# Projection of q and k in two passes of 1024 tokens, the first by seven products of halves

## The chip, the cores and the metric

The kernel runs on one core of a Trainium2 chip. The metric is the device time of one execution in microseconds; the time of a kernel is the median of its runs. TensorE (PE) multiplies matrices, VectorE (DVE), ScalarE (ACT) and GpSimd (POOL) work on elements, and SyncE (SP), ScalarE and GpSimd issue DMAs, each in the order of the program.

## The reference

Two blocks read the same x (2048 tokens of 1024) and are mixed by a gate. Block A is attention with 32 heads of 32; block B chooses one of 64 experts for each of 32 heads by a product of keys.

```
qkv = x @ wqkv                                   # 1024 -> 3 x 1024: q, k, v of 32 heads
p   = softmax(q k^T * 32**-0.5);  a = (p v) @ wo
s1, s2 = (x w_q) split in halves, times k1, k2   # 8 scores each, the largest of each chosen
b   = sum over heads of gelu(x . u[e]) v[e]      # e: the chosen expert of the head
g   = sigmoid(sum(x * gate_w));   out = g * a + (1 - g) * b
```

This text is about q and k alone: x (2048 x 1024) times the first 2048 columns of `wqkv`.

## The kernel before

One program, one core. All products that need more accuracy than a rounded operand gives are made of two parts: `split(hi, lo, src)` (L92 to L94) copies a tile into a rounded type on ScalarE (L93: the high part) and subtracts it from the source on VectorE (L94: the low part). A product is then three matmuls: high by high, high by low, low by high. A matmul takes a 128x128 block of weights and 512 tokens.

The stages follow one another on TensorE: projection of q and k, router (`router_mm`, L394), v (`values`, L636), v again as seven products of halves for most tokens (`Halves.product`, L617), attention (scores L969, exponentials L979, p v L990), and the output projection.

Projection. x comes transposed, in eight block rows of 128 by 2048, and stays in SBUF as `xh` and `xl` (four tiles of 512 tokens each). The weights of q and k are 16 chunks of 128 columns: chunk c of q, then chunk c of k. The first two chunks run row by row while x arrives: for each block row `kc`, 24 matmuls into eight banks (L213). Their weights come on ScalarE's queue in four pieces (block rows 0, 1, 2 to 3, 4 to 7). The order on ScalarE and VectorE is that of the program: for `kc` 1, `split_x(1)` and then the third piece of the weights; for `kc` 2, `split_x(2)` and then the fourth piece; so both stand ahead of the next row of x.

The other 14 chunks run one after another: a chunk has four blocks of 512 tokens, each of 24 matmuls into one bank (L329). After a block, `evac` splits the bank into parts (L93, L94), takes the maximum of the high part (L141) and puts off the two stores to DRAM to the next eviction. Between the blocks stand other pieces of work, in a table by block number: `fold` (L274) folds the router's weights with its keys on TensorE, `gate` (L313) adds x times the gate's weights on VectorE, and near the end the router's folded weights are loaded and split. Eight banks of PSUM (`bk0` to `bk7`) are handed out in turn by `bank()`.

The loop over chunks before (L322 to L334; `whl` holds a chunk's two parts, `load_w` and `split_w` fetch and split the next):

```
for k, (w, c) in enumerate(chunks):
    hi, lo = whl.pop((w, c))
    for n in range(NQ):
        ps = bank()
        for kc in range(KC):
            for a, b, first, last in ((hi, xh, kc == 0, False), (hi, xl, False, False),
                                      (lo, xh, False, kc == KC - 1)):
                nc.tensor.matmul(ps, a[:, kc, :], b[n][:, kc, :], start=first, stop=last)
        if n == 0 and 0 < k < len(chunks) - 1:
            split_w(*chunks[k + 1])
        ...
        evac(w, c, n, ps, pair(ev, "", 1))
```

On GpSimd stand only the router's products (L408, L421, L434) and DMAs, the folds' stores among them.

`Halves` (before, after the router) makes a product of a 2x2 arrangement of halves by seven products in place of eight: A are the stationary blocks, B the moving ones.

```
FACTORS = dict(P1=("A11", "B11"), P2=("A12", "B21"), P3=("S4", "B22"), P4=("A22", "T4"),
               P5=("S1", "T1"), P6=("S2", "T2"), P7=("S3", "T3"))
S1 = A21 + A22, S2 = S1 - A11, S3 = A11 - A21, S4 = A12 - S2
T1 = B12 - B11, T3 = B22 - B12, T2 = B22 - T1, T4 = B21 - T2     # each overwrites one of its inputs
C11 = P1 + P2; u2 = P1 + P6; u3 = u2 + P7; u2 += P5; C22 = u3 + P5; C12 = u2 + P3; C21 = u3 + P4
```

Each product is 12 matmuls (four block rows, three parts) into one bank. S and T are sums of raw halves and are split into parts after that.

Of the kernel before, what the change touches and what calls it, by code (L numbers as in the profile page):

```python
# [16 lines left out]
S = 2048  # L17
# [14 lines left out]
def gated_mha_peer_kernel(ctx, tc, xT, wqkv, wv, wo, wq, k12, ug, v, out):  # L32
# [62 lines left out]


    xp = Pool("xp")

    xh, xl = ([xp.tile([128, KC, 512], F32R, name=f"x{part}{n}") for n in range(NQ)] for part in "hl")
    ps1 = Pool("ps1", space=PSUM)  # L100
    bank_no = [0]

    def bank():
        i = bank_no[0] % 8
        bank_no[0] += 1
        return ps1.tile([128, 512], F32, name=f"bk{i}")

    amax = const.tile([128, 2, KC], F32, name="amax")
    wp = Pool("wp", bufs=2)
    ev = Pool("ev", bufs=3)  # L110
    xr = Pool("xr", bufs=4)

    wraw, whl = {}, {}

    def load_w(which, c):
        t = wp.tile([128, KC, 128], F32, name="wraw", bufs=1)
        dma(t, wqkv[which * 8 + c].rearrange("p (k m) -> p k m", k=KC))
        wraw[which, c] = t

    def split_w(which, c):  # L120
        t = wraw.pop((which, c))
        hi = wp.tile([128, KC, 128], F32R, name="whi")
        lo = wp.tile([128, KC, 128], F32R, name="wlo")
        split(hi, lo, t)
        whl[which, c] = hi, lo
# [9 lines left out]
    def evac(which, c, n, ps, parts):  # L135

        m = parts[0].shape[1] // 512
        hi, lo = (t[:, n % m * 512:(n % m + 1) * 512] for t in parts)
        split(hi, lo, ps)
        mx = ev.tile([128, 1], F32, name="m", bufs=8)  # L140
        nc.vector.tensor_reduce(mx, hi.bitcast(F32), axis=AX.X, op=OP.max, apply_absolute_value=True)  # L141
        am = amax[:, which, c:c + 1]
        if n == 0:
            nc.vector.tensor_copy(am, mx)
        else:
            nc.vector.tensor_max(am, am, mx)
        store_parts()
        if n % m == m - 1:
            for dst, t in zip(QKD[which], parts):
                stores.append((dst[128 * c:128 * c + 128, (n + 1 - m) * 512:(n + 1) * 512], t))  # L150

    def pair(pool, name, m):
        return [pool.tile([128, m * 512], F32R, name=part + name) for part in ("hi", "lo")]
# [13 lines left out]
    x_t = {}  # L167

    def load_x(kc, pieces=1):
        t = xr.tile([128, S], F32, name="xraw")  # L170
        n = S // pieces
        for i in range(pieces):
            dma(t[:, i * n:(i + 1) * n], xT[kc * 128:(kc + 1) * 128, i * n:(i + 1) * n])
        x_t[kc] = t

    def split_x(kc):
        for n in range(NQ):
            split(xh[n][:, kc, :], xl[n][:, kc, :], x_t[kc][:, n * 512:(n + 1) * 512])

    w0 = []  # L180
    for w in range(2):
        w0.append([xr.tile([128, KC, 128], F32, name="w0raw", bufs=2),
                   wp.tile([128, KC, 128], F32R, name="whi"), wp.tile([128, KC, 128], F32R, name="wlo")])

    def load_w0(k0, k1):
        for w in range(2):
            dma(w0[w][0][:, k0:k1, :],
                wqkv[w * 8, :, k0 * 128:k1 * 128].rearrange("p (k m) -> p k m", m=128), nc.scalar)

    def split_w0(k0, k1):  # L190
        for raw, hi, lo in w0:
            split(hi[:, k0:k1, :], lo[:, k0:k1, :], raw[:, k0:k1, :])

    load_w0(0, 1)
    load_x(0, 4)
    load_w0(1, 2)
    load_x(1, 2)
    split_w0(0, 1)
    split_x(0)
    load_w0(2, 4)  # L200
    load_x(2, 2)
    load_w0(4, KC)
    load_x(3, 2)
    split_w0(1, 2)
    b0 = {(w, n): bank() for w in range(2) for n in range(NQ)}


    for i in range(9):
        nc.tensor.matmul(b0[1, NQ - 1][:, :128], ident, ident, start=True, stop=True)

    def mm0(w, n, kc, i):
        a, b = ((1, xh), (1, xl), (2, xh))[i]
        nc.tensor.matmul(b0[w, n], w0[w][a][:, kc, :], b[n][:, kc, :],  # L213
                         start=(kc == 0 and i == 0), stop=(kc == KC - 1 and i == 2))

    for kc in range(KC):
        if kc:
            split_x(kc)
        if kc in (1, 2):
            split_w0(2 * kc, 2 * kc + 2 if kc == 1 else KC)  # L220
        if kc + 4 < KC:
            load_x(kc + 4)
        if kc == KC - 5:
            load_w(0, 1)
        if kc == KC - 1:
            split_w(0, 1)
            load_w(1, 1)

            xr.close()
            ev0 = Pool("ev0")  # L230
        order = [(n, i) for i in range(3) for n in range(NQ)]
        if kc in (0, KC - 1):
            order = [(n, i) for n in range(NQ) for i in range(3)]
        for w in range(2):
            for n, i in order:
                mm0(w, n, kc, i)
            if kc == KC - 1:
                parts = pair(ev0, str(w), NQ)
                for n in range(NQ):
                    evac(w, 0, n, b0[w, n], parts)  # L240

    split_w(1, 1)
    load_w(0, 2)
    ev0.close()
    wqp = Pool("wqp", bufs=4)


# [315 lines left out]

    class Halves:

# [856 lines left out]
```

## Time and profile before

| | us |
|---|---|
| median of 3 runs | 1852.09 (1851.99 to 1853.69) |
| the profiled execution | 1852.0 |
| its span, first to last instruction | 1850.2 |
| first matmul of L213 | 6.67 |
| first matmul of L329 | 51.94 |
| first matmul of L394 (router) | 391.02 |

In the rows, a line number is one of the kernel before. A row of the timeline has the start and the length in us, the engine, line, operation, tile written and read, and behind it in brackets how long the engine sat idle before it and what ended that. A row of groups has the count, busy time, mean length in ns and idle time before. A row of stretches has the bounds, the length, and the busy time and count of TensorE, its weight loads, VectorE, ScalarE and GpSimd, then TensorE's granted clock, the DMA share and GB/s. Matmuls overlap, so the length of one is not its cost.

### The profile page before, as it was taken

How to read it: one execution, taken by the hardware profiler on the slowest of the kernel's cores; microseconds unless marked ns; L12 is line 12 of the kernel's file. 1: busy time of each engine (PE TensorE's matmuls, PEld its weight loads, DVE VectorE, ACT ScalarE, POOL GpSimd, SP SyncE). 2: the span in 40 equal slices, each digit the busy share in tenths (PEclk: the TensorE clock that was granted, in tenths of full speed). 3: DMA queues.
4: the chain of work that ended last, by engine and by line, in shares of the span. 5: the costliest groups of instructions: out<-in, count | busy, mean ns of one | idle time of the engine just before them, and what ended most of it. 6: DMA issues, size and time to landing. Idle time of an engine off the chain costs nothing.

```text
span 1850.2 us, 26111 instructions
## 1 busy us (share of the span) xinstructions
PE 1842.3 (100%) x10127; PEld 1128.0 (61%) x10127; DVE 1365.0 (74%) x1219; ACT 1197.8 (65%) x1491; POOL 172.3 (9%) x218
## 2 busy tenths in 40 slices
PE   9999999999999999999999999999999999999999
PEld 7877777887888744444444444444444444447887
DVE  4522224978887788888888888888888888895684
ACT  4211111201233399999999999999999999993221
POOL 0000000026401100000000000000000000001000
PEclk9999999999999999999999999999999999999999
DMA  5777784423237787767777777877777777866961
GB/s 216 283 255 252 273 291 135 133 69 104 80 119 249 253 184 160 174 157 173 164 174 176 167 183 159 191 162 182 174 165 173 162 179 164 181 146 192 279 185 63
DMA packets 122150, 332.10 MB, mean 179 GB/s; under 512 B 15924, under 2 KB 56260, under 8 KB 97768
## 3 DMA queue, kind: packets, MB, share of 16 engines
q1 hardware_dynamic: 85112, 180.72, 32.0%
q0 software_dynamic: 17904, 112.99, 28.3%
q10 hardware_dynamic: 19008, 36.71, 6.3%
q8 instruction: 80, 1.31, 0.3%
q14 instruction: 46, 0.38, 0.1%
HBM read 158.65 MB, written 72.10 MB: 125 GB/s over the span
## 4 chain that ended last, share of the span: by engine, by line
PE 94%; DMA 4%; SPq 1%; ACT 1%; issue 0%; DVE 0%; ACTq 0%; DVEq 0%
PE ring L969 27%; PE o L990 25%; PE bk L329 17%; PE bk L617 6%; PE pa L617 5%; PE bk L394 5%; PE bk L636 2%; PE bk L213 2%; DMA accd<-P 2%; PE bk L274 2%; PE ring L1003 1%; DMA wo_raw<-t1l 1%; SPq L75 1%; DMA out<-rb 1%; PE pa L1181 1%; DMA at<-atd 0%
## 5 line engine op out<-in xcount | busy, mean ns | idle before, releaser
L979 ACT ACTIVATE P<-ring 128x512 f32<-128x512 f32 (+2 forms) x1030 | 912.5, 985 | 15.1 <-DMA accd<-P 2.3
L1019 DVE TENSOR_TENSOR acc<-acc,P 128x2048 f32<-128x2048 f32 x319 | 731.0, 2292 | 74.2 <-ACT P L979 48.6
L990 PE MATMUL o<-P,V 128*32 128x512 f32 x3840 | 464.8, 599 | 0.0
L969 PE MATMUL ring<-Q,K 98*128 98x512 f32 x1024 | 272.3, 407 | 0.2
L969 PE MATMUL ring<-z,z 98*128 98x512 f32 x1020 | 271.3, 407 | 0.3 <-ACT P L979 0.2
L969 PEld LDWEIGHTS ring<-Q,K 98*128 98x128 f32 x1024 | 181.9, 188 | 144.7 <-ACT P L979 73.8
L969 PEld LDWEIGHTS ring<-z,z 98*128 98x128 f32 x1020 | 181.2, 188 | 143.8 <-ACT P L979 71.6
L990 PEld LDWEIGHTS o<-P,V 128*32 128x32 f32 x3840 | 98.8, 109 | 223.1 <-issue 214.4
L93 ACT ACTIVATE hi<-bk 128x512 fp32r<-128x512 f32 x64 | 37.6, 598 | 243.1 <-PE bk L329 231.8
L94 DVE TENSOR_TENSOR lo<-bk,hi 128x512 fp32r<-128x512 f32 x64 | 44.1, 690 | 182.7 <-ACT hi L93 178.1
L329 PE MATMUL bk<-xh,whi 128*128 128x512 f32 x448 | 176.2, 393 | 0.1
L329 PE MATMUL bk<-xh,wlo 128*128 128x512 f32 x448 | 174.4, 389 | 0.0
L329 PE MATMUL bk<-xl,whi 128*128 128x512 f32 x448 | 174.4, 389 | 0.0
L1012 POOL DMA_DIRECT2D accd<-P x95 | 81.5, 858 | 930.6 <-ACT P L979 400.9
L1017 DVE TENSOR_TENSOR acc<-P,P 128x2048 f32<-128x2048 f32 x32 | 73.4, 2292 | 74.1 <-ACT P L979 74.1
L329 PEld LDWEIGHTS bk<-xh,whi 128*128 128x128 f32 x448 | 84.1, 188 | 24.2 <-issue 6.7
L329 PEld LDWEIGHTS bk<-xh,wlo 128*128 128x128 f32 x448 | 84.1, 188 | 17.7
L329 PEld LDWEIGHTS bk<-xl,whi 128*128 128x128 f32 x448 | 84.2, 188 | 17.0
L1022 DVE TENSOR_TENSOR acc<-acc,accd 128x2048 f32<-128x2048 f32 x32 | 73.1, 2284 | 0.0
L979 ACT ACTIVATE accd<-ring 128x1024 f32<-128x1024 f32 (+2 forms) x64 | 62.3, 1034 | 1.7 <-PE ring L969 1.6
L617 PE MATMUL pa<-woh,acc 128*128 128x512 f32 x192 | 62.6, 390 | 0.3 <-DVE acc L94 0.3
L398 ACT ACTIVATE xu<-bk 128x64 f32<-128x64 f32 x16 | 3.6, 224 | 76.5 <-PE bk L394 71.6
(247 smaller groups left out, 1864.7 us busy)
## 6 DMA issues: line engine op xcount, KB each, us to landing
accd<-P POOLq DMA_DIRECT2D x95, 1024.0 KB, 7.4
wqt<-in_wq SPq DMA_DIRECT2D x32, 1024.0 KB
z<-kdh SPq DMA_DIRECT2D x32, 256.0 KB
z<-qdh SPq DMA_DIRECT2D x32, 256.0 KB
V<-vd SPq DMA_DIRECT2D x32, 256.0 KB
K<-kdh SPq DMA_DIRECT2D x32, 256.0 KB
Q<-qdh SPq DMA_DIRECT2D x32, 256.0 KB
od<-osb SPq DMA_DIRECT2D x32, 256.0 KB
```

The lines of the kernel that those rows point to most:

```text
L93: nc.scalar.activation(hi, src, AF.Copy)
L94: (on or nc.vector).tensor_tensor(out=lo, in0=src, in1=hi.bitcast(F32), op=OP.subtract)
L329: nc.tensor.matmul(ps, a[:, kc, :], b[n][:, kc, :], start=first, stop=last)
L394: nc.tensor.matmul(ps, a[t // 4][:, kc, tok], b, start=first, stop=last)
L617: nc.tensor.matmul(ps, self.a[a][i][:, k, :], self.b[b][j][k], start=(not first and k == 0 and i == j == 0), stop=(k == HC - 1 and i == 1))
L969: on_ring(nc.tensor.matmul(ring[:, i, :], K[:98, kt * 128:(kt + 1) * 128], Q[:98, qc * 512:(qc + 1) * 512], start=True, stop=True), i)
L979: on_ring(nc.scalar.activation(P[h, kt][:, q0 * 512:(q0 + m) * 512].rearrange("p (a m) -> p a m", a=m), ring[:, i:i + m, :], AF.Exp, scale ...
L990: nc.tensor.matmul(O[h][32 * qc:32 * qc + 32, :], Vt[g][:, kt, 32 * j:32 * j + 32], p[:, qc * 512:(qc + 1) * 512], start=(kt == 0), stop=( ...
L1012: nc.gpsimd.dma_start(ACCD[h], P[h, kt], accum_op=OP.add)
L1017: nc.vector.tensor_add(ACC[h], P[h, 0], P[h, kt])
L1019: nc.vector.tensor_add(ACC[h], ACC[h], P[h, kt])
L1022: nc.vector.tensor_add(ACC[h], ACC[h], ACCD[h])
```

## The change

The first pass covers tokens 1024 to 2047. Chunk 0 of q and k runs as before, row by row, for these tokens (four banks, 12 matmuls per block row). Then come seven units: unit c makes chunk c of q and of k together by the seven products of `Halves`. A11 and A12 are the two halves (512 of the 1024 input features each) of q's chunk, A21 and A22 those of k's; B11 and B12 are tokens 1024 to 1535 and 1536 to 2047 of the first 512 features, B21 and B22 of the others. The sums S run on GpSimd in every unit, 512 wide. T1, T2 and T4 run on GpSimd once, 2048 wide, T3 on VectorE. While a unit runs, the operands of the next are split, each when the product that last used its place is issued.

The second pass covers tokens 0 to 1023 for all 16 chunks in blocks of 24 matmuls as before; x of these tokens is loaded during units 6 and 7, the weights are loaded and split again, and x of the first pass is loaded and split again, since its raw blocks were overwritten by the T. The gate's terms, its sums on TensorE (before: in the router stage) and most folds move into the second pass, 12 folds into units 2 to 5. `evac` writes each block's maximum to a place of its own, and one reduction at the end replaces the running maximum.

The core of the diff (`Halves` itself moves up; its `sums` takes an engine and the places to write to):

```diff
+    def evac_hi(which, c, n, src):
+        hi, lo = (ev.tile([128, 512], F32R, name=part) for part in ("hi", "lo"))
+        nc.scalar.activation(hi, src, AF.Copy)
+        late.append((which, c, n, src, hi, lo))
+
+    def evac_lo():
+        which, c, n, src, hi, lo = late.pop(0)
+        nc.vector.tensor_tensor(out=lo, in0=src, in1=hi.bitcast(F32), op=OP.subtract)
+        nc.vector.tensor_reduce(amax4[:, which, c, n:n + 1], hi.bitcast(F32), axis=AX.X, op=OP.max,
+                                apply_absolute_value=True)
+        store_parts()
...
+    load_x(raws[0], 0, 0, T0, 2)
+    load_w0(1, 2)
+    load_x(raws[0], 0, 1, T0, 2)
+    split_w0(0, 1)
+    split_x(0)
+    load_w0(2, 4)
+    load_x(raws[0], 0, 2, T0)
+    load_w0(4, KC)
+    load_x(raws[0], 0, 3, T0)
+    split_w0(1, 2)
+    for k in range(HC):
+        load_x(raws[1], 1, k, T0)
+    w1 = [load_w(w, 1) for w in range(2)]
...
+    for kc in range(KC):
+        if kc:
+            split_x(kc)
+        if kc == 1:
+            split_w0(2, 4)
+        if kc == 2:
+            split_w0(4, KC)
+        if kc == 4:
+            t1 = x_sum("T1", nc.gpsimd)
+        order = [(n, i) for i in range(3) for n in (2, 3)]
+        if kc in (0, KC - 1):
+            order = [(n, i) for n in (2, 3) for i in range(3)]
+        for w in range(2):
+            for n, i in order:
+                mm0(w, n, kc, i)
...
+    set_rows(1)
+    t3 = x_sum("T3", nc.vector)
+    for name in ("S3", "S1"):
+        hq.sums(name, nc.gpsimd)
+    for name in ("A11", "A12"):
+        hq.parts(name)
+    for name in ("S2", "S4"):
+        hq.sums(name, nc.gpsimd)
+    t2, t4 = (x_sum(name, nc.gpsimd) for name in ("T2", "T4"))
+    x_parts("T3", t_tile("xh0"), t3)
+    hq.parts("S4")
+    x_parts("T1", t_tile("xl0"), t1)
+    hq.parts("S3")
...
+    evac_first(2)
+    hq.parts("S1")
+    x_parts("T2", t_tile("xh1"), t2)
+    hq.parts("S2")
+    evac_first(2)
+    x_parts("T4", t_tile("xh3"), t4)
+    hq.parts("A22")
+
+    def qk_unit(c, order, nxt, hooks):
+        p, done = {}, set()
+        k0 = 3 if c == 1 else 0
+        for k, name in enumerate(order):
+            if nxt and k == k0:
+                set_rows(nxt)
+                for s in ("S3", "S1"):
+                    hq.sums(s, nc.gpsimd)
+            p[name] = hq.product(name)
+            if name == "P1":
+                c1 = cp.tile([128, 512], F32, name="c1")
+                nc.scalar.activation(c1, p[name], AF.Copy)
+                if late:
+                    evac_lo()
+            if nxt and k == k0:
+                hq.parts("A11")
+                hq.sums("S2", nc.gpsimd)
...
+            if name == "P6":
+                u2, u3, u5 = (cp.tile([128, 512], F32, name=name) for name in ("u2", "u3", "u5"))
+                tt(u2, c1, p["P6"])
+                tt(u3, u2, p["P7"])
+                tt(u2, u2, p["P5"])
+                tt(u5, u3, p["P5"])
+                evac_hi(1, c, 3, u5)
+            if "P6" in p:
+                for q, (o, w, n) in (("P2", (c1, 0, 2)), ("P3", (u2, 0, 3)), ("P4", (u3, 1, 2))):
+                    if q in p and (w, n) not in done:
+                        done.add((w, n))
+                        tt(o, o, p[q])
+                        evac_hi(w, c, n, o)
+                        evac_lo()
+            if nxt and k >= k0:
+                for q in ("P7", "P5", "P6", "P2", "P3", "P4"):
+                    if q in p and q not in done:
+                        done.add(q)
+                        hq.parts(hq.FACTORS[q][0])
+                        if q == "P2":
+                            hq.sums("S4", nc.gpsimd)
...
+            store_parts()
+            for f, *args in hooks.get(name, ()):
+                f(*args)
...
+    hooks[7] = {"P1": [(load_raws, 1, "xh2")], "P7": [(w_chunk, 0, 0, 0), (again, 0, 0, "xh0")],
+                "P5": [(again, 0, 1, "xl0")], "P6": [(w_chunk, 1, 0, 1)],
+                "P2": [(again, 1, 0, "xh1")], "P3": [(again, 1, 1, "xl1")]}
+    for c in range(1, KC):
+        qk_unit(c, ("P1", "P2", "P3", "P7", "P5", "P6", "P4") if c == 1 else
+                ("P1", "P7", "P5", "P6", "P2", "P3", "P4"), c + 1 if c < KC - 1 else None, hooks[c])
...
+    between[1] = [(again2, 3, 1, "xl3", 1)]
+    between[2] = [(gate_raw, 3, 1, 1), (load_again, 2, 1, 1)]
...
+    order = [(0, 0), (1, 0), (0, 1), (1, 1)] + [(k, n) for k in range(2, len(chunks)) for n in range(2)]
+    for blk, (k, n) in enumerate(order):
+        w, c = chunks[k]
+        t = pairs[k % 2]
+        ps = bank()
+        for kc in range(KC):
+            for a, b, first, last in ((0, 0, kc == 0, False), (0, 1, False, False),
+                                      (1, 0, False, kc == KC - 1)):
+                nc.tensor.matmul(ps, t[:, kc // HC, a, kc % HC], x_at(b, n, kc), start=first, stop=last)
+        if blk == 2 or (blk > 3 and n == 0 and k < len(chunks) - 1):
+            nxt = 2 if blk == 2 else k + 1
+            w_chunk(*chunks[nxt], nxt % 2)
...
+        evac(w, c, n, ps)
```

`x_sum` makes one T in place over one of its inputs, `x_parts` splits it (2048 wide), `again` and `again2` split a reloaded block of x (2048 wide), `gate_raw` and `gate_part` add its gate terms (four operations of 512), `w_chunk` splits a reloaded chunk of weights (1024 wide).

507 lines of the change are left out of this document (285 added, 222 removed).

## The prediction

> **What bounds the kernel now.** I read the page first (busy shares, slices, the chain that ended last), then TensorE's waits and the timeline of the projection, then VectorE's, ScalarE's and GpSimd's rows, and last the loads of the start.
>
> ```profile
> span 1850.2 us, 26111 instructions
> PE 1842.3 (100%) x10127; PEld 1128.0 (61%) x10127; DVE 1365.0 (74%) x1219; ACT 1197.8 (65%) x1491; POOL 172.3 (9%) x218
> PE ring L969 27%; PE o L990 25%; PE bk L329 17%; PE bk L617 6%; PE pa L617 5%; PE bk L394 5%; PE bk L636 2%; PE bk L213 2%; DMA accd<-P 2%; PE bk L274 2%; PE ring L1003 1%; DMA wo_raw<-t1l 1%; SPq L75 1%; DMA out<-rb 1%; PE pa L1181 1%; DMA at<-atd 0%
> ```
>
> The chain is TensorE almost throughout, and the projection of q and k (L213 and L329) is 19% of it. Where TensorE stands in that stretch:
>
> ```profile
> L213 PE MATMUL bk<-xh,whi x64: 388/389/503, 6.7 to 51.0; 128*128 128x512 f32 x64
> 51.48 0.39 PE L213 MATMUL bk<-xh,wlo 128*128 128x512 f32 x1
> 51.94 0.50 PE L329 MATMUL bk<-xh,whi 128*128 128x512 f32 x1
> L329 PE MATMUL bk<-xh,whi x448: 389/389/499, 51.9 to 390.3; 128*128 128x512 f32 x150
> 391.02 0.39 PE L394 MATMUL bk<-wph,xh 128*128 128x512 f32 x1
> 293.21 97.97 PE bk L329 x432
> PE bk L213 <- ACT xh L93: 1.1, 1, 1.1
> ```
>
> Each kind of matmul has 64 (L213) or 448 (L329) instructions and there are three kinds, so 192 + 1344 = 1536 in all, from 6.7 us to 391.0. A row says 389 ns for one, but they overlap: the chain holds 432 of them in 97.97 us, that is 0.2268 us each. This, not 0.389, is what a removed matmul is worth. The first 192 take 43.5 us at that pace and end at about 51.7, so the start loses 1.5 us; after it TensorE has no wait worth naming. The work here is bound by TensorE and the rest has room, so the question is whether the others keep up when it gets shorter.
>
> **What goes.** Chunks 1 to 7 (of q and of k) in the first pass cost 7 products of 12 matmuls in place of 4 blocks of 24: 84 for 96. Chunk 0 keeps its 96 and the second pass has 16 x 2 x 24 = 768. Together 96 + 588 + 768 = 1452, 84 fewer: 84 x 0.2268 = **19.0 us** less. The folds, their transposes and the gate's sums only move. One product lasts 2.7 us and one unit (a chunk of q and k) 19.0.
>
> **What comes, and on which engine.**
>
> ```profile
> 22.45 12.13 DVE L94 TENSOR_TENSOR xl<-xraw,xh 128x512 fp32r<-128x512 f32 x20
> 21.71 10.52 ACT L93 ACTIVATE xh<-xraw 128x512 fp32r<-128x512 f32 x20
> L623 DVE TENSOR_TENSOR xh<-xh,bk 128x512 f32<-128x512 f32 x41 | 27.3, 683 | 0.7 <-PE bk L617 0.2
> 51.20 0.68 DVE L94 TENSOR_TENSOR lo<-bk,hi 128x512 fp32r<-128x512 f32 x1
> 51.80 0.68 DVE L141 TENSOR_REDUCE m<-hi 128x1 f32<-128x512 f32 x1
> L94 DVE TENSOR_TENSOR xl<-xl,xl 128x2048 fp32r<-128x2048 f32 x3 | 6.9, 2286 | 0.0
> L408 POOL TENSOR_TENSOR eq<-eq,e x16: 1287/1294/3243, 398.7 to 486.5; 128x512 f32<-128x512 f32 x16
> L434 POOL TENSOR_TENSOR pq<-eq,p x32: 637/664/1156, 405.3 to 491.5; 128x256 f32<-128x256 f32 x32
> ```
>
> In a row VectorE does a 512-wide subtraction every 0.60 us (12.13 / 20) and ScalarE a copy every 0.52. An eviction costs VectorE 1.2 us (0.60 each for subtraction and maximum), a 2048-wide split 2.3. A steady unit asks VectorE for 7 low parts (4.2), 7 sums with a bank (4.2) and 4 evictions (4.8): 13.2 of 19.0 us. GpSimd's four sums a unit cost 1.29 each, 5.2. Its 2048-wide sums (T1, T2, T4) no row shows: by the step from 256 to 512 (0.63 us) one is 1.29 + 6 x 0.63 = 5.1; the lower end is four times the 1.06 of the next fence, 4.2; I take 4.6, for the fixed part of an instruction is paid once.
>
> [...]
>
> These sums are not free beside VectorE:
>
> ```profile
> 443.89 1.30 POOL L408 TENSOR_TENSOR eq<-eq,e 128x512 f32<-128x512 f32 x1 [1.47 <-DVE eq L407]
> 443.98 3.35 DVE L94 TENSOR_TENSOR xh<-xh,xh 128x2048 fp32r<-128x2048 f32 x1 [0.17 <-ACT xh L93]
> 456.31 2.29 DVE L94 TENSOR_TENSOR xl<-xl,xl 128x2048 fp32r<-128x2048 f32 x1
> 456.51 3.24 POOL L408 TENSOR_TENSOR eq<-eq,e 128x512 f32<-128x512 f32 x1 [0.93 <-DVE eq L407]
> 432.79 0.68 DVE L440 TENSOR_REDUCE packed<-pq 128x16 f32<-128x512 f32 x1
> 432.98 1.29 POOL L408 TENSOR_TENSOR eq<-eq,e 128x512 f32<-128x512 f32 x1 [2.74 <-DVE eq L407]
> ```
>
> Where GpSimd began first, VectorE's split took 3.35 in place of 2.29 (1.06 more); where VectorE began first, GpSimd's took 3.24 in place of 1.29. The two never advance together when both read two operands of SBUF. With a reduction beside it GpSimd loses nothing. So a split's low part and a sum of halves follow one another. For long GpSimd instructions no row shows whether they let go in between.
>
> [...]
>
> **Start.** Each block row of x is now half as long, so TensorE uses it up in 12 matmuls (2.7 us) instead of 24, while chunk 0's weights stay 1 MB in the same four pieces.
>
> ```profile
> 16.19 0.42 ACT L93 ACTIVATE whi<-w0raw 128x256 fp32r<-128x256 f32 x1 [1.82 <-DMA w0raw<-in_wqkv]
> 21.17 0.63 ACT L93 ACTIVATE whi<-w0raw 128x512 fp32r<-128x512 f32 x1 [1.96 <-DMA w0raw<-in_wqkv]
> 7.46 0.34 ACTq L75 DMA_DIRECT2D w0raw<-in_wqkv  x1
> 10.00:20.00 10.00, 9.96 (x42) 7.37 (x41) 6.59 (x13) 5.93 (x13) 0.00 (x0) 1.00 1.00 378
> ```
>
> Now the third piece lands at 16.2 and the fourth at 21.2, hidden by 43 us of matmuls. The DMA share is 1.00 there, so they come little earlier: they are issued about 1.1 us sooner (two copies fewer ahead of 7.46), and I take 15.2 and 19.2. ScalarE splits them ahead of x's rows 2 and 3, so TensorE, which has used up rows 0 and 1 by 13.2, starts row 2 at 16.3 and row 3 at 20.6, and with waits for low parts ends chunk 0 at about 34.9; unhindered it is 6.7 + 21.8 = 28.5. That is 6.5 lost against 1.5 today: **+5.0**. Bounds: pieces 4.7 us earlier, +0.3; at the times of today, +7.
>
> **The first unit.** Row 3 of x is split from 20.5 on, and five rows of two subtractions each make 6.0, so VectorE is done with row 7 at 26.5; T1, queued on GpSimd, gets between at the earliest there. From then on one after the other: T1 4.6, the S3 sum 1.2, T3 on VectorE (it overwrites what T1 reads) 2.3, the low parts of A11 and A12 1.2, the S1 sum 1.2, T3's low part 2.3, the S2 and S4 sums 2.5, T2 4.6 (queued straight behind S4, while S4's high part is still being made), S4's low part 0.6: 20.5, so 47.0, with gaps 47.5. TensorE is through P1 and P2 at 40.8 and needs that part in P3. VectorE then still has T1's low part 2.3, S3 0.6, S1 0.6, T2 2.3, S2 0.6, T4 2.3, A22 0.6 and chunk 0's four evictions 4.8, 14.1 in all, and is held about 3.5 by the T4 sum (4.6, of which 1.1 run beside evictions, which read a bank): 65.1. P4 needs A22 from its third matmul on; the unit ends at 67.7. Unhindered it is 34.9 + 19.0 = 53.9: **+13.8** (bounds 0, if nothing were held, as the same work in two queues ends ahead of P4, and 15.5 with 5.1 for a long sum).
>
> **The second unit.** VectorE enters it with all of chunk 2's low parts ahead of the four sums that set free the banks of P7, P5 and P6; P5 of this unit needs the bank of the last P2, whose sum comes at 77, and TensorE is there at 73. With what S2 costs behind it: **+5.0** (0 to 6). Units 3 to 7 have 13.2 + 5.2 = 18.4 of 19.0 (21.7 with folds) even if every sum shuts VectorE out, so nothing.
>
> **The second pass.** In unit 7 VectorE has two weight splits (1.2 each), four of 2048 (9.2), 4.2 of sums and five evictions (6.0), 21.8 of 19.0, and then four reloaded blocks and their gate terms:
>
> ```profile
> L313 DVE SCALAR_TENSOR_TENSOR zacc<-xl,ugr,zacc 128x512 f32<-128x512 f32 x32 | 21.9, 746 | 0.0
> 150.00:300.00 150.00, 150.00 (x766) 110.44 (x765) 39.41 (x75) 25.90 (x40) 4.50 (x6) 1.00 0.75 254
> 300.00:400.00 100.00, 100.00 (x443) 82.81 (x442) 77.62 (x160) 19.15 (x37) 1.26 (x1) 1.00 0.42 123
> ```
>
> A block lasts 5.4 us and asks for 1.2 + 0.6 (weights) + 2.3 or 4 x 0.66, at most 4.4, so it catches up slowly; the low part of the third chunk's weights waits behind this queue. **+2.5** (0 to 5). The 16 MB loaded again (all of x and of the weights of q and k once more) run beside 254 and 123 GB/s (last column) where 378 were moved at the start: nothing. Attention and all later stages start later or earlier by the same amount.
>
> **Sum.** 5.0 + 13.8 + 5.0 + 2.5 - 19.0 = +7.3. The profiled execution took 1852.0 us (span 1850.2), as the median of the runs, 1852.09: **1859.3**.
>
> **The rivals.** 0.2% (3.7 us) is about what a measurement of this kernel can tell from no change.
> 1. Forecast, slower: own range 1856 to 1866. Chance 0.50.
> 2. Faster: GpSimd's long sums let VectorE in, or T1 slips in while the start waits for weights, so that S4's low part is there at 40.8 and nothing of the 13.8 and 5.0 remains. Then -19.0 + 5.0 + 0 to 2.5: 1838.0 to 1840.5. For it: VectorE and ScalarE alone have room (13.2 of 19.0). Against it: 3.35 and 3.24. Chance 0.30.
> 3. Between: the arbiter serves VectorE first at each gap, P3 waits half as long and VectorE enters unit 2 without its queue: 5.0 + 7 + 4 + 2.5 - 19.0 = -0.5, 1851.5, within 0.2%. Chance 0.15.
> 4. Slower still: the start takes the times of today and the long sums 5.1: 7 + 15.5 + 6 + 5 - 19.0 = +14.5, 1866.5. Chance 0.05.
> That the products are not fewer I give no chance: the loops count them.
>
> **How the numbers follow.** Faster 0.30, same 0.15, slower 0.55. The range runs from rival 2 with a start better by 1 us, 1837, to the forecast's upper end next to rival 4, 1866. The likeliest case alone is 1856 to 1866.
>
> **What would show it.** 1452 three-part matmuls at 0.227 us between starts; chunk 0 ending near 35 us; TensorE waiting for low parts in P3, P5 and P4 of the first unit, 13.8 us in all; VectorE rows of over 3 us and GpSimd rows of over 5 between 26 and 65 us. Wrong, if the first unit takes about 19 us, or if stalls return in units 3 to 7.

## The result and the profile after

| | before | after |
|---|---|---|
| median of the runs (us) | 1852.04 | 1871.03 (1867.51 to 1873.48, 4 runs) |
| the same, measured once more later | 1850.87 | 1868.79 (1865.67 to 1869.75, 5 runs) |
| profiled execution, span (us) | 1852.0, 1850.2 | 1867.51, 1865.7 |

The changed kernel is slower: ratio 1.0102, 95% interval 1.0082 to 1.0122, and 1.0093 (1.0079 to 1.0107) the second time. The forecast was 1859.3 and at most 1866. The direction was right, the size was not. Of the profiled executions the difference is 15.5 us, of which 7.3 were forecast.

The page of the changed kernel, its first lines:

```profile
span 1865.7 us, 26221 instructions
PE 1836.6 (98%) x10043; PEld 1115.5 (60%) x10043; DVE 1460.2 (78%) x1237; ACT 1245.2 (67%) x1545; POOL 227.5 (12%) x249
```

TensorE's busy time fell by 5.7 us (1842.3 before) and its share from 100% to 98%, while VectorE gained 95 us of work and GpSimd 55. So TensorE now waits. Where, is read from busy time by stretch. The columns are: window, its length, busy time (and instructions) of PE, PEld, DVE, ACT and POOL, granted clock, DMA share, GB/s. The windows of before are chunk 0, the rest of the projection, and the router:

```profile
6.00:51.94 45.94, 44.94 (x193) 35.81 (x193) 24.26 (x42) 22.14 (x45) 0.00 (x0) 1.00 0.52 194
51.94:391.02 339.08, 339.08 (x1632) 262.38 (x1633) 148.93 (x282) 63.24 (x105) 6.19 (x8) 1.00 0.68 227
391.02:480.34 89.32, 89.02 (x397) 72.17 (x396) 71.51 (x146) 12.05 (x22) 50.16 (x55) 1.00 0.21 66
```

Those of after are chunk 0, unit 1, unit 2, units 3 to 7, the second pass, and the router:

```profile
6.00:35.74 29.74, 25.69 (x97) 19.02 (x97) 24.93 (x26) 13.63 (x25) 12.24 (x5) 0.94 0.61 227
35.74:65.99 30.25, 23.33 (x86) 17.84 (x84) 27.84 (x19) 12.44 (x16) 14.87 (x6) 0.89 0.34 105
65.99:92.47 26.48, 23.06 (x110) 16.09 (x109) 19.47 (x33) 8.34 (x14) 5.47 (x4) 1.00 0.63 231
92.47:199.22 106.75, 105.60 (x506) 81.80 (x504) 81.06 (x109) 40.03 (x64) 25.55 (x20) 1.00 0.85 279
199.22:399.79 200.57, 198.18 (x957) 149.97 (x956) 114.01 (x151) 56.13 (x75) 3.77 (x5) 1.00 0.83 260
399.79:494.50 94.71, 91.56 (x390) 73.67 (x388) 72.16 (x150) 14.19 (x29) 49.66 (x55) 0.96 0.21 68
```

The router starts at 399.79 in place of 391.02: 8.8 us later. It then takes 94.71 in place of 89.32, 5.4 more, though the gate's sums have left it. Everything behind it adds 1.3. The same kernel was profiled once more later (span 1866.3 us); there the router starts at 401.82 and takes 93.78, so a stretch of a single profile can be 1 to 2.5 us off. The windows of after show who is busy while TensorE is not: in unit 1 VectorE works 27.84 of 30.25 us. And the granted clock, 1.00 in all windows of before, is 0.94, 0.89 and 0.96 in three of them.

What TensorE waits for, from the same kernel (engine, tile, line; who ended it; sum, times, longest):

```profile
PE bk L149 <- DVE e L95: 5.3, 2, 4.2
PE bk L378 <- DVE xl L95: 3.4, 2, 2.2
PE bk L691 <- ACT wph L94: 2.7, 2, 1.9
```

L378 is chunk 0, L149 the products, L691 the router. The rows of VectorE behind the first two, all of them low parts of splits (the second row is the first of the eight subtractions in the row above it):

```profile
16.98 11.45 DVE L95 TENSOR_TENSOR xl<-xl,xl 128x512 fp32r<-128x512 f32 x8
16.98 5.07 DVE L95 TENSOR_TENSOR xl<-xl,xl 128x512 fp32r<-128x512 f32 x1
36.99 4.46 DVE L95 TENSOR_TENSOR e<-wraw,e 128x512 fp32r<-128x512 f32 x1 [1.84 <-ACT e L94]
41.37 6.66 DVE L95 TENSOR_TENSOR xl<-xh,xl 128x2048 fp32r<-128x2048 f32 x1
```

and what GpSimd does beside them:

```profile
16.54 4.96 POOL L398 TENSOR_TENSOR xh<-xh 128x2048 f32<-128x2048 f32 x1 [15.45 <-DMA xl<-in_xT]
36.25 4.64 POOL L398 TENSOR_TENSOR xl<-xl,xh 128x2048 f32<-128x2048 f32 x1
40.97 4.90 POOL L398 TENSOR_TENSOR xl<-xl 128x2048 f32<-128x2048 f32 x1
```

A subtraction that takes 0.69 us alone takes 5.07 beside T1 and ends (22.05) half a microsecond behind it (21.50). Another takes 4.46 and ends (41.45) half a microsecond behind the sum T2 (40.89); one of 2.29 takes 6.66 and ends 2.2 us behind T4. Each was started while GpSimd was in a long sum, and got its own time after that sum. That is what the prediction read from 3.35 and 3.24, at four times the length.

The router's weights are the part that no step of the prediction has. ScalarE's splits of the folded weights, the four of the eight that wait for a load:

```profile
394.78 0.58 ACT L94 ACTIVATE wph<-wpr 128x448 fp32r<-128x448 f32 x1 [3.45 <-DMA wpr<-wpd]
400.34 0.58 ACT L94 ACTIVATE wph<-wpr 128x448 fp32r<-128x448 f32 x1 [3.75 <-DMA wpr<-wpd]
405.20 0.58 ACT L94 ACTIVATE wph<-wpr 128x448 fp32r<-128x448 f32 x1 [2.90 <-DMA wpr<-wpd]
407.52 0.58 ACT L94 ACTIVATE wph<-wpr 128x448 fp32r<-128x448 f32 x1 [1.60 <-DMA wpr<-wpd]
```

The first router tile needs all eight parts, one after the other, from 399.8 on, and the last is split at 407.5. There are two buffers for the loads, and the next load is asked for only after a split.

### The profile page after: what moved, and what is told of

It reads as the page before. It is cut to its first block, busy times and chain, and to the rows that moved or that the text cites. A ratio compares the mean times of both kernels' runs of the same rounds, so it can differ in the third digit from the quotient of the medians.

```text
span 1865.7 us, 26221 instructions
## 1 busy us (share of the span) xinstructions
PE 1836.6 (98%) x10043; PEld 1115.5 (60%) x10043; DVE 1460.2 (78%) x1237; ACT 1245.2 (67%) x1545; POOL 227.5 (12%) x249
## 3 DMA queue, kind: packets, MB, share of 16 engines
q8 instruction: 80, 1.31, 0.3%
## 4 chain that ended last, share of the span: by engine, by line
PE 71%; issue 10%; DMA 8%; DVE 6%; POOL 3%; ACT 2%; SPq 1%; ACTq 0%; DVEq 0%; POOLq 0%
PE ring L1192 26%; PE o L1213 24%; PE bk L644 8%; PE pa L149 5%; DMA accd<-P 3%; PE bk L691 3%; PE bk L149 2%; PE ring L1226 1%; DMA wraw<-in_wqkv 1%; DVE e L95 1%; DVE u L155 1%; PE bk L297 1%; POOL wraw L131 1%; DVE xl L95 1%; POOL eq L705 1%
## 5 line engine op out<-in xcount | busy, mean ns | idle before, releaser
L235 ACT ACTIVATE hi<-bk 128x512 fp32r<-128x512 f32 x36 | 21.1, 595 | 112.0 <-PE bk L644 103.0
L644 PE MATMUL bk<-xh,e 128*128 128x512 f32 x384 | 94.3, 394 | 1.3 <-DVE e L95 1.3
L644 PE MATMUL bk<-xl,e 128*128 128x512 f32 x384 | 92.6, 389 | 1.1 <-DVE xl L95 1.1
L149 PE MATMUL bk<-xh,e 128*128 128x512 f32 x336 | 84.3, 405 | 8.5 <-DVE e L95 5.3
L95 DVE TENSOR_TENSOR e<-wraw,e 128x512 fp32r<-128x512 f32 (+3 forms) x66 | 62.8, 956 | 30.9 <-ACT e L94 30.0
L644 PEld LDWEIGHTS bk<-xh,e 128*128 128x128 f32 x384 | 71.0, 188 | 22.9 <-issue 5.0
L644 PEld LDWEIGHTS bk<-xl,e 128*128 128x128 f32 x384 | 72.0, 188 | 16.5 <-DVE xl L95 1.5
L149 PEld LDWEIGHTS bk<-xh,e 128*128 128x128 f32 x336 | 64.5, 195 | 27.7 <-DVE e L95 6.5
L241 DVE TENSOR_TENSOR lo<-bk,hi 128x512 fp32r<-128x512 f32 x36 | 24.8, 689 | 68.4 <-ACT hi L235 68.4
L94 ACT ACTIVATE e<-wraw 128x512 fp32r<-128x512 f32 (+3 forms) x66 | 46.0, 702 | 33.5 <-POOL wraw L131 13.3
```

The source lines that it names most:

```text
L94: nc.scalar.activation(hi, src, AF.Copy)
L95: (on or nc.vector).tensor_tensor(out=lo, in0=src, in1=hi.bitcast(F32), op=OP.subtract)
L149: nc.tensor.matmul(ps, self.a[a][i][:, k, :], self.b[b][j][k], start=(not first and k == 0 and i == j == 0), stop=(k == HC - 1 and i == 1))
L644: nc.tensor.matmul(ps, t[:, kc // HC, a, kc % HC], x_at(b, n, kc), start=first, stop=last)
```

## The experiments

All are variants of the changed kernel. Its own median was 1871.0 and 1868.8 at two times, so a difference of 2 us between medians is not told apart. The verdicts rest on the stretches of the trace, one profile of each kernel; those of the two profiles of the changed kernel differ by up to 2.5 us (unit 2: 26.48 and 28.97).

### All sums on VectorE

```diff
-            t1 = x_sum("T1", nc.gpsimd)
+            t1 = x_sum("T1", nc.vector)
...
-        hq.sums(name, nc.gpsimd)
+        hq.sums(name, nc.vector)
```

and so at the other places of S1 to S4, T2 and T4.

> All sums of pass 1 (T1, T2, T4, S1 to S4) are made by VectorE in place of GpSimd. Theory of the shared path (an addition on GpSimd and an operation of VectorE with two operands in SBUF hold each other up, as in the rows 41.37 6.66 and 36.99 4.46 of the changed kernel): VectorE's subtractions of chunk 0 and unit 1 run at 0.6 and 2.2 us each, the first product starts at about 32 us in place of 35.7, unit 2 starts at about 58 in place of 66.0, the time falls by 7 to 9 us to 1862 to 1864. Rival (VectorE just has too much to do in a fixed order, and GpSimd relieves it): 20 us more in VectorE's row up to the end of unit 1, unit 2 starts at 68 or later, the time is 1873 or more.

Measured: 1860.13 us (1857.08 to 1862.94), ratio to before 1.0044 (1.0027 to 1.0061). Chunk 0, unit 1 and the second pass, and VectorE's rows at the end of chunk 0:

```profile
6.00:31.15 25.15, 24.72 (x96) 19.38 (x97) 20.91 (x32) 13.71 (x25) 0.00 (x0) 1.00 0.73 267
31.15:55.97 24.82, 21.07 (x85) 15.37 (x84) 23.62 (x23) 12.44 (x16) 0.00 (x0) 1.00 0.39 114
187.86:391.74 203.88, 198.71 (x958) 149.89 (x956) 115.79 (x154) 56.22 (x75) 3.75 (x5) 1.00 0.83 258
```
```profile
17.96 1.29 DVE L95 TENSOR_TENSOR xl<-xl,xl 128x512 fp32r<-128x512 f32 x2
19.16 2.29 DVE L398 TENSOR_TENSOR xh<-xh 128x2048 f32<-128x2048 f32 x1
21.37 3.69 DVE L95 TENSOR_TENSOR xl<-xl,xl 128x512 fp32r<-128x512 f32 x6
```

VectorE does more and is done earlier: the same eight subtractions and the sum T1 take 7.1 us where the subtractions alone took 11.45 beside GpSimd. Chunk 0 ends 4.6 us earlier, unit 1 is 5.4 shorter (4.0 and 4.1 against the second profile of the changed kernel), and VectorE is busy 23.6 in place of 27.8 us in it. The rival, that GpSimd relieves VectorE, is out. Of the 11.4 us won by the start of the second pass, 3.3 are lost in that pass (203.88 for 200.57): its third block waits for x and takes 10.18 us. In the two profiles of the changed kernel that block takes 6.90 and 9.67, so how much of the 3.3 belongs to this edit is open.

### Only the long sums, or only the short ones

```diff
-            t1 = x_sum("T1", nc.gpsimd)
+            t1 = x_sum("T1", nc.vector)
...
-    t2, t4 = (x_sum(name, nc.gpsimd) for name in ("T2", "T4"))
+    t2, t4 = (x_sum(name, nc.vector) for name in ("T2", "T4"))
```

> Only the three long sums (T1, T2, T4, 128x2048) are made by VectorE; the four short ones per chunk (128x512) stay on GpSimd. If the cost goes by the time in which GpSimd holds VectorE, the long sums held it for 4.96, 4.64 and 4.90 us against 2.29 us each on VectorE itself, 7.6 us in all, the short ones of the first unit for about 6 against 2.8: two thirds of the gain of 10.9 us of the kernel with all sums on VectorE, so about 7 us faster than the changed kernel, 1864 us, and the first product at 31 to 32 us. Rival (only the sum of both counts, since the chain behind the short sums sets unit 1's end): under 3 us, 1868 or more.

Measured: 1864.37 us, ratio 1.0070 (1.0053 to 1.0087). The first product starts at 33.2 and unit 1 still takes 30.24 us.

The other half, T1, T2, T4 on GpSimd and S1 to S4 on VectorE:

```diff
-        hq.sums(name, nc.gpsimd)
+        hq.sums(name, nc.vector)
```

> Only the short sums (S1 to S4, 128x512) are made by VectorE; the long ones stay on GpSimd. By the time held: a third of 10.9 us, about 3.5 us faster than the changed kernel, 1867 to 1868 us, and the first product at 35 to 36 us as in the changed kernel, since T1 is still beside the subtractions of chunk 0. Rival (the short sums set unit 1's end, through S4 and S3): 6 us or more, 1865 or less.

Measured: 1862.23 us (1861.26 to 1866.18), ratio 1.0054 (1.0038 to 1.0071). VectorE's rows and GpSimd's where unit 1 begins, at 35.07:

```profile
31.12 4.99 DVE L131 TENSOR_TENSOR wraw<-wraw 128x512 f32<-128x512 f32 x1
36.04 5.58 DVE L95 TENSOR_TENSOR e<-wraw,e 128x512 fp32r<-128x512 f32 x2
```
```profile
30.62 4.94 POOL L398 TENSOR_TENSOR xl<-xl,xh 128x2048 f32<-128x2048 f32 x1 [7.10 <-DVE xh L398]
35.64 4.83 POOL L398 TENSOR_TENSOR xl<-xl 128x2048 f32<-128x2048 f32 x1
```

A sum of 0.69 us on VectorE takes 4.99 and ends at 36.11, behind GpSimd's at 35.56; the two subtractions then take 5.58 in place of 1.29, behind the next one. So GpSimd did not let go during these long sums of 4.94 and 4.83 us.

The division of the gain that I expected, two thirds to the long sums, isn't borne out: by the medians each half gives 4 to 9 us and together they would exceed the whole (9 to 11). What GpSimd still did held what was moved to VectorE (4.99 us for a sum of 0.69). How the gain divides stays open: the profiled run of the second kernel, 1866.18, is the longest of its four.

### A sum on GpSimd that nobody needs

The kernel with all sums on VectorE, and in addition:

```diff
         if kc == 4:
+            nc.gpsimd.tensor_tensor(out=raw_x("xh0")[:, :, :512], in0=half(0, 1), in1=half(0, 1), op=OP.add)
             t1 = x_sum("T1", nc.vector)
```

> The kernel with all sums on VectorE, and one addition of 128x2048 more on GpSimd at the time of T1, into a place that is empty then; nobody uses its result, and nothing waits for it but the later owner of the place. Theory that GpSimd's addition holds VectorE whatever it works on: the eight subtractions 128x512 of the second half of chunk 0, 5.0 us in all without it, take about 10 us again, the first product starts 3 to 5 us later than 31.2 and the time is 3 to 5 us above that kernel's 1860.1 us, so 1863 to 1865 us. Rival (the gain came only from the waits for GpSimd's results, not from its running beside): 5.0 us, 31.2 and 1860 again.

Measured: 1859.35 us (1858.47 to 1861.85), ratio 1.0043 (1.0027 to 1.0058); the profiled run is the longest, 1861.85. GpSimd, VectorE, and chunk 0:

```profile
14.44 4.08 POOL L416 TENSOR_TENSOR xh<-xh 128x2048 f32<-128x2048 f32 x1 [13.35 <-DMA wraw<-in_wqkv]
```
```profile
16.32 2.74 DVE L95 TENSOR_TENSOR e<-wraw,e 128x512 fp32r<-128x512 f32 x1 [1.27 <-ACT e L94]
```
```profile
6.00:34.76 28.76, 24.77 (x97) 19.11 (x98) 24.31 (x32) 14.97 (x27) 4.08 (x1) 0.94 0.64 234
```

The sum ran 2 us earlier than T1 had, beside the split of the weights, and not beside the eight subtractions, which keep their rate (1.28 and 3.69). The split it met took 2.74 in place of 0.69 and ended half a microsecond behind it. Chunk 0 ends 3.6 us later than without, some of that at the half clock (0.94). So a sum whose result nobody awaits held VectorE as well: the 2.74 us are the 2.20 that were left of the sum, and half a microsecond. The eight subtractions that the expectation named were not the ones that met the sum, so that part of it was not tested; chunk 0 ends later as expected. The median shows nothing of it: 1859.4 against 1860.1. In the profiled executions the second pass starts 3.2 us later (191.02 for 187.86), but the first of these is the longest of its kernel's four runs and the other the shortest of its four. Why the medians agree stays open.

### The weights of chunk 0 early

```diff
-    load_w0(1, 2)
...
+    for k0, k1 in one[1:]:
+        load_w0(k0, k1)
     load_x(raws[0], 0, 0, T0, 2)
```

> All loads of the weights of chunk 0 are issued ahead of ScalarE's first split. Theory of the shared path: what held chunk 0 was GpSimd's T1 beside VectorE's subtractions, so the first product still starts at 34.5 to 36 us and the time is within 1 us of 1871. Rival (late weight pieces behind ScalarE's splits): the first product starts at about 32.5 us, the time falls by 3 us to 1868. Third outcome: the weights take transfer time from x, and the first chunk starts later by 1 us or more.

Measured: 1868.10 us (1865.91 to 1873.63), ratio 1.0089 (1.0070 to 1.0108). Chunk 0 and unit 1:

```profile
6.00:32.19 26.19, 23.87 (x96) 19.00 (x97) 22.82 (x28) 14.70 (x27) 10.67 (x4) 1.00 0.72 277
32.19:65.45 33.26, 25.24 (x86) 18.96 (x84) 30.26 (x20) 12.43 (x16) 18.19 (x7) 0.85 0.32 95
```
```profile
17.66 5.13 DVE L95 TENSOR_TENSOR xl<-xl,xl 128x512 fp32r<-128x512 f32 x1
```

Chunk 0 ends 3.5 us earlier, as the rival had it, but unit 1 is 3.0 longer and ends at 65.45 in place of 65.99 (64.04 in the second profile of the changed kernel). The end of unit 1 is set by VectorE's and GpSimd's queue; TensorE may arrive when it likes. The eight subtractions take as long in all as before (11.52 us), but two of them are done before T1 holds the third (the row at 17.66); in the changed kernel T1 held the first (16.98, 5.07 us). So TensorE has 33 matmuls left at 24.5 us, where it had 45 left at 23.8, and it runs the last rows at the full clock (1.00 for the window; 0.94 in the changed kernel). T1 beside the subtractions therefore costs chunk 0 time by which of them it meets, and not by their sum alone.

### The folds of the second pass earlier

```diff
-    for i, b in enumerate((10, 13, 16, 19, 22, 25, 27)):
+    for i, b in enumerate((10, 12, 14, 16, 18, 20, 22)):
...
-    between[28] += [(open_router,)]
+    between[24] += [(open_router,)]
     for kc in range(KC):
-        between[29 + kc // 3] += [(split_wp, kc)]
+        between[26 + kc // 2] += [(split_wp, kc)]
```

> The folds of pass 2 follow each other every two blocks (10 to 22 in place of 10 to 27), and the router's weights are opened at block 24 and split at blocks 26 to 29 in place of 28 and 29 to 31. Theory that the router's start waits for its late weights: the router stage shrinks from 94.7 us to about 88.4, the time falls by about 6 us to 1865. Rival (the stage is longer for another reason, such as the subtraction order on VectorE or the evictions; or the folds delay the blocks as much when they are denser): the router stage stays above 92 or pass 2 grows by what the router gains, the time is within 2 us of 1871.

The second spacing is 10, 12, 14, 17, 19, 22, 24, with the opening at 26 and the splits at `27 + (kc + 1) // 2`:

> The folds of pass 2 at blocks 10, 12, 14, 17, 19, 22, 24, the router's weights opened at 26 and split at 27 to 31. If the first fold experiment lost its 3.4 us in pass 2 to folds that followed each other too closely for their loads (blocks 16 and 18 at 9.88 and 9.24 us in place of 8.24), pass 2 is back at 201 to 202 us and the router stage stays at about 88: 5 to 6 us faster than the changed kernel, 1865 us. Rival (the 3.4 us come from elsewhere): pass 2 stays at 203 or more and the time at 1867.

Measured: 1866.85 us, ratio 1.0078 (1.0061 to 1.0094), and 1864.41 us, ratio 1.0064 (1.0048 to 1.0081). The second pass and the router, first spacing, then the second:

```profile
197.90:401.91 204.01, 198.51 (x958) 149.93 (x956) 117.65 (x161) 58.97 (x83) 3.85 (x5) 1.00 0.80 259
401.91:490.00 88.09, 87.79 (x389) 72.08 (x388) 69.32 (x142) 11.41 (x21) 49.73 (x55) 1.00 0.21 67
```
```profile
200.81:403.30 202.49, 199.92 (x958) 151.09 (x956) 117.19 (x159) 58.14 (x81) 3.84 (x5) 0.99 0.82 262
403.30:491.40 88.10, 87.80 (x390) 72.10 (x388) 70.00 (x144) 12.13 (x23) 49.73 (x55) 1.00 0.21 67
```

The router's stage is 88.1 in both, 6.6 us shorter than in the changed kernel and 1.2 shorter than before (the gate's sums). So its excess came from the late weights, with the half clock behind the waits for them. With folds every second block the second pass is 3.4 us longer than in the first profile of the changed kernel. By the starts of its matmuls, block 16 takes 9.88 us for 8.24, of which 1.3 are a fold that waits for its load. Block 18, which the text on the second spacing counts as another such wait, takes 9.24 because the gate's sums stand in it beside the folds; no wait shows there. The third block, which waits for x, takes 9.15 us for 6.90. With the second spacing no fold waits, and the third block takes 10.44 us. But the unaltered kernel's second profile has 9.67 there, and a second pass as long as this one:

```profile
199.58:401.82 202.24, 199.82 (x958) 151.21 (x956) 114.23 (x152) 56.49 (x76) 3.78 (x5) 0.99 0.82 258
```

So the 1.9 us that the pass is longer with the second spacing need not come from the edit.

### Products of the identity against the half clock

```diff
             ps = (bank or self.bank)()
+            for i in range(self.warm.pop(name, 0)):
+                nc.tensor.matmul(ps[:, :128], ident, ident, start=True, stop=True)
```

with `dict(P7=16, P4=8)`, and the same with 10 ahead of the first router tile.

> Products of the identity, thrown away, are put ahead of P7 (16) and P4 (8) in unit 1 and ahead of the first router tile (10), so that TensorE is busy while it would wait. Theory that the half clock after a wait is a cost of its own: the windows with granted clock 0.5 at 49.3, 63.0 and 407.7 us go, with 1.7 us each, so the time falls by 3 to 5 us to 1866 to 1868. Rival (in these windows the operands come late anyway, so the rate does not matter): less than 1 us in all, 1870 to 1872; and if the extra products end after the operands are there, 1 to 2 us slower.

Measured: 1878.31 us, ratio 1.0140 (1.0123 to 1.0156). The edit also reached the units of v: 24 products, 48 records, and 167.4 us between values and scores in place of 162.6. That is 5 of the 7 us that it is slower; the rest lies in its early stretches (unit 2 ends at 96.04 in place of 92.47). Without the products in v:

> As the kernel with products of the identity, but without the extra products that it had also put into the later units of v (48 records, 5.0 us between values and scores): 16 ahead of P7 and 8 ahead of P4 of unit 1 of q and k, 10 ahead of the first router tile. By what the first one showed (unit 1 ended at 65.2 in place of 66.0 us, so its operands set its end): within 1.5 us of the changed kernel, 1869 to 1873 us. Rival (the half clock is a cost of its own): 1868 or less.

Measured: 1865.54 us, ratio 1.0081 (1.0065 to 1.0096): on the rival's side, 1868 or less. But its first product comes at 34.07 in place of 35.74, though the edit alters nothing ahead of it, so the two profiles differ by more than the edit. I therefore put the two places apart, with the changed kernel unaltered beside them:

> The changed kernel once more, unaltered, as the measure for the two that run beside it: 1871 us as before, 1868 to 1873.

> The changed kernel with 10 products of the identity ahead of the first router tile and nowhere else. Theory that the half clock after the wait there costs time of its own: the first two tiles take 7.2 and 5.5 us behind 2.2 us of extra products, 14.9 in place of 17.5, so 2 to 3 us less than the unaltered one beside it. Rival (the late weights set the end of these tiles): within 1 us of it.

> The changed kernel with 16 and 8 products of the identity ahead of P7 and P4 of unit 1 and nowhere else. Theory of a cost of its own: the 3.4 us windows at the half clock in unit 1 go, and 2 to 3.5 us with them. Rival (the low parts of VectorE set the end of unit 1): unit 1 ends within 1 us of 66.0 and the time is within 1 us of the unaltered one beside it.

Measured: 1868.79 unaltered, 1867.90 with products ahead of the router (ratio to before 1.0093, 1.0078 to 1.0109), 1867.89 with those in unit 1 (1.0094, 1.0078 to 1.0109). No difference can be told. A window of the changed kernel at the half clock, at the router:

```profile
407.70:411.10 3.40, 2.81 (x6) 2.06 (x7) 2.20 (x23) 0.77 (x3) 0.00 (x0) 0.50 0.00 2
```

Unit 1 with extra products, and the router's stage with the extra products counted in:

```profile
35.63:65.86 30.23, 27.74 (x134) 22.02 (x133) 27.83 (x19) 12.55 (x16) 14.54 (x6) 0.94 0.34 105
```
```profile
400.02:492.32 92.30, 90.64 (x409) 74.25 (x408) 72.17 (x150) 14.19 (x29) 49.73 (x55) 1.00 0.22 70
```

Unit 1 ends at 65.86, as in the changed kernel; but only one of the two windows at the half clock went (granted clock 0.94 for the unit, 0.89 in the changed kernel). The kernel with products in all three places has none in unit 1 (1.00) and ends it at 63.75; the second profile of the unaltered kernel has 0.88 there and ends it at 64.04. So VectorE sets its end, and no cost of the clock shows there. The router's stage is 2.4 us shorter than 94.71 (and 1.5 shorter than in the unaltered kernel measured beside it, 93.78): the last weights had come while TensorE still ran slowly. By these single profiles the half clock costs 1.5 to 2.4 us at the router, behind the wait that brought it; the time of the whole kernel does not show it (1867.90 and 1868.79).

### All causes taken away

All sums on VectorE, the second spacing of the folds, and the two blocks of x for the second quarter split one behind the other:

```diff
-                "P2": [(again, 1, 0, "xh1")], "P3": [(again, 1, 1, "xl1")]}
+                "P2": [(again, 1, 0, "xh1"), (again, 1, 1, "xl1")]}
```

and, in the first of two such kernels, T2 and T4 made just ahead of their own splits, and the low parts of S4 and S3 made one split earlier.

> All sums on VectorE, each long one just ahead of its own split; the folds and the router's weights as in the kernel with the second spacing; and both blocks of x for the second quarter of pass 2 are split one behind the other at P2 of unit 7. If the causes are separate, the gains add: 10.9 us from the sums, 5 to 6 from the folds, 1.5 to 3 from the order of the long sums (P3 of unit 1 at 2.7 in place of 4.3 us), 2 to 3 from the block of pass 2 that waits for x (10.2 us with all sums on VectorE): 1848 to 1852 us, at or below the kernel before. Rival (what is gained early is given back at the next wait, as when the weights of chunk 0 came early): 1855 or more.

Measured: 1854.85 us (10 runs), ratio 1.0019 (1.0009 to 1.0029). Making T2 and T4 so late was a mistake. VectorE in unit 1:

```profile
40.56 2.28 DVE L398 TENSOR_TENSOR xl<-xl,xh 128x2048 f32<-128x2048 f32 x1
44.83 2.29 DVE L95 TENSOR_TENSOR xh<-xl,xh 128x2048 fp32r<-128x2048 f32 x1 [1.98 <-ACT xh L94]
```

Between a sum and its low part ScalarE must make the high part, and VectorE, in order, stands idle 1.98 us; it did so twice, and unit 1 took 31.2 us. In the second kernel the sums and low parts are back where they were, and two steps of the second pass are in another order:

```diff
+    load_w(0, 1, single=True)
     load_again(3, 1, 1)
     load_again(3, 0, 2)
...
-    between[1] = [(again2, 3, 1, "xl3", 1)]
-    between[2] = [(gate_raw, 3, 1, 1), (load_again, 2, 1, 1)]
+    between[2] = [(again2, 3, 1, "xl3", 1), (gate_raw, 3, 1, 1), (load_again, 2, 1, 1)]
...
-    load_w(*chunks[2], single=True)
```

> As the kernel with all causes taken away, but the long sums T2 and T4 are again made one behind the other ahead of the splits (that kernel waited twice 2 us between a sum and its split, and unit 1 took 31.2 us in place of 24.8), the weights of chunk 1 are asked for ahead of the router's x, and the first block of the router's x is split one block later (block 4 took 9.25 us). Gains that add: 5 to 6 us from unit 1, 2 to 3 from block 4, so 1846 to 1850 us, below the kernel before. Rival (given back at the next wait): 1853 or more.

Measured: **1846.56 us** (11 runs, 1845.90 to 1851.49), ratio to before 0.9978 (0.9969 to 0.9987): faster than both kernels. Unit 1, the second pass and the router:

```profile
30.89:55.72 24.83, 21.11 (x86) 15.38 (x84) 23.63 (x23) 12.43 (x16) 0.00 (x0) 1.00 0.39 117
189.38:386.77 197.39, 197.39 (x957) 150.21 (x956) 116.76 (x159) 57.94 (x81) 3.83 (x5) 1.00 0.82 269
386.77:474.90 88.13, 87.83 (x390) 72.16 (x389) 70.02 (x144) 12.12 (x23) 49.78 (x55) 1.00 0.21 67
```

The second pass has no wait left (PE busy 197.39 of 197.39), where it had 203.88 with the sums on VectorE alone. The gains add here, as expected: 10.4 us by the span of the kernel with all sums on VectorE, from there 6.5 in the second pass and 5.1 at the router (93.2 to 88.1), less 1.8 in unit 2, make 20.2; the span fell by 21.0. Units 1 and 2 still take about 6 us each more than their matmuls and folds need (24.83 for 19.0, 28.15 for 21.8).

## Why the prediction was wrong, point by point

| step | forecast | after | after, second profile |
|---|---|---|---|
| matmuls left out | -19.0 | -19.0 (products at 0.227 us) | -19.0 |
| chunk 0 | +5.0, ends 34.9 | +5.7, first product 35.74 | +5.1, 35.12 |
| unit 1 | +13.8 | +11.2 (30.25 for 19.0) | +9.9 (28.92) |
| unit 2 | +5.0 | +4.7 (26.48, of which 2.8 are folds) | +7.2 (28.97) |
| units 3 to 7 | 0 | +1.2 (106.75; 105.51 in the fastest kernel) | +1.1 (106.57) |
| second pass | +2.5 | +3.2 (200.57; 197.39 in the fastest kernel) | +4.9 (202.24) |
| router's start | 0 | +6.6 (94.71; 88.13 in the fastest kernel) | +5.7 (93.78) |

In the first profile 1.3 us are added behind the router, and 0.6 in the projection is not assigned (0.8 and 0.4 in the second). The 1.2 us of the gate's sums moved from the router's stage into the second pass.

**The mechanism was right.** GpSimd's sums beside VectorE cost about half of the 19.0 us that the products save: with the sums on VectorE, 8.7 to 10.9 us of the medians come back. To the start of the router the forecast sum was +7.3; it was +8.8 (+10.8 in the second profile), 1.2 of it the gate's sums.

**The step that failed** is the sentence "The folds, their transposes and the gate's sums only move", in what goes. They were costed at nothing without naming what hid them. In the kernel before, the router's weights were opened at block 38 of 56, and the eight loads through two buffers were over when the router began. In the second pass the last folds stand at block 27 of 32 and the weights are opened at block 28. The first two loads are asked for at 375.8 us, the other six only from 391.6 on, each behind a split; the chain that ended last holds three of them, with 3.17, 4.28 and 5.14 us. The prediction priced the moved steps' engines and not the chain behind them: store, load, two buffers, split. That is 6.6 of the 8.2 us missing in the profiled execution (5.7 of 8.8 in the second profile). Of the 6.6, 2.9 are idle time of TensorE and 3.7 are slower matmuls (91.56 us busy, 87.83 in the fastest kernel), at the half clock behind the waits (granted 0.50 from 407.0 to 413.8). The experiments with earlier folds and loads showed it: 88.1 in place of 94.7.

**Right in size, wrong in its working: chunk 0.** The late weights were to cost 6.5 us. They came earlier than I took, at or ahead of my early bound:

```profile
9.41 0.42 ACT L94 ACTIVATE e<-wraw 128x256 fp32r<-128x256 f32 x1 [0.27 <-DMA wraw<-in_wqkv]
14.50 0.63 ACT L94 ACTIVATE e<-wraw 128x512 fp32r<-128x512 f32 x1 [1.26 <-DMA wraw<-in_wqkv]
```

The third pieces were split at 9.4 and 11.2 and the fourth at 12.6 and 14.5, for 15.2 and 19.2 forecast. So T1 could start at 16.5, not behind row 7 at 26.5, and it held VectorE in the middle of chunk 0. The second rival had seen T1 slip in at the start, as a gain; it did spare the wait at P3 (S4's low part was there at 41.5, for 47.5 forecast), but chunk 0 paid for it. The waits at P7 and P4 came: 4.2 us at P7, for S3's low part stood on VectorE behind T1's, which T4's sum held to 48.0. TensorE's idle time in unit 1 is 6.9 us (30.25 less 23.33 busy), where 13.8 were forecast as waits; most of the other 4.3 is the half clock (two windows of 3.4 us at a granted clock of 0.50). So unit 1 came out near its forecast partly by luck.

**The rival that let VectorE in** is out by the rows 4.46, 6.66 and 4.99. The price of a long sum, 4.6 us taken between 4.2 and 5.1, was 4.64 to 4.96 in the changed kernel; the sum that nobody needs took 4.08. The fixed part of an instruction, for which I took 4.6 between the two, was my estimate; no row shows it.

**The half clock** was in no step. In the changed kernel it came behind waits, in five windows of 3.4 us at a granted clock of 0.50 (from 24.7, 48.6 and 62.3 us, and two on end from 407.0), and by single profiles it cost 1.5 to 2.4 us at the router. The windows follow one wait of 4.2 us, but also shorter ones with a single matmul between, as these in P4 of unit 1:

```profile
60.32 0.50 PE L149 MATMUL bk<-xh,e 128*128 128x512 f32 x1 [1.31 <-DVE xh L95]
62.00 9.62 PE L149 MATMUL bk<-xh,e 128*128 128x512 f32 x34 [1.18 <-DVE e L95]
```

**The rest**, 3.5 us between the profiled run (1867.51) and the median of its four, is the spread of this kernel: five later runs have 1868.79. The range ended at 1866 because the only case above it had a chance of 0.05; no case stood for a cost that had not been thought of.

## What to carry to other kernels

Work moved from a busy VectorE to an idle GpSimd was no relief here, where both read two operands from SBUF: giving VectorE all of it back made unit 1 4.1 to 5.4 us shorter. A step that "only moves" has a chain behind it; count the buffers and landings between it and its user before costing it at nothing. And a gain ahead of a queue that sets the end (3.5 us at chunk 0) is given back at that end, so the first thing to look for is which engine's row has no gap.

## What of the hardware I had not expected

As the forecast took it, and now measured: the additions of 128x2048 on GpSimd (4.64 to 4.96 us) held VectorE's two-operand work that was started beside them to their end: 0.69 us became 4.46, 4.99 and 5.07, 2.29 became 6.66. Not expected: TensorE ran at half its clock (granted 0.50) in windows of 3.4 us after a wait of 4.2 us, two waits of 2.20 and 1.18 or of 1.31 and 1.18, or, at the router, 1.94 and shorter ones, one matmul every 0.427 us in place of 0.227; the kernel before had no such window in the stretches shown.
